# Block B's q and k: two of four x tiles by seven block products in place of eight

## The chip, the cores and the metric

The kernel runs on one core of a Trainium2 chip. The metric is the device time of one execution in microseconds (us), the median of several. Five engines work side by side, each in the order of its own queue: TensorE (PE; its weight loads are listed as PEld), VectorE (DVE), ScalarE (ACT), GpSimd (POOL) and SyncE (SP), which issues nearly all DMAs. PSUM has eight banks of 128 x 512 numbers here; PE writes into them, and ACT and DVE read them out.

## The reference

Two attention blocks, A and B, run on inputs of their own, and their outputs stand side by side. Both have a sequence of 2048, a width of 640 and 32 heads of 20.

```
qkv = (x @ wqkv).reshape(B, S, 3, H, Dh)          # both blocks
A:  logits over 8 dilated neighbours (idx = pos - 2*w), softmax, weighted sum, @ wo
B:  softmax(q @ k^T * Dh**-0.5) @ v over all 2048 positions, @ wo
out = concatenate([a, b], axis=-1)
```

The change touches only block B's q and k: `x @ wqkv[:, :1280]`, which is 10 feature blocks of 128 by 2048 positions, with a contraction of 640.

## The kernel before

All numbers are float32. For a product in float32 precision each operand is split into a high part (rounded) and a low part (operand less high part), and each chunk of 128 of the contraction takes three matmuls, `PASSES`: high by high, high by low, low by high. A split is one ACT copy (the high part) and one subtraction, mostly on DVE (`a_split`, line 217).

The stages follow one another on PE:

1. Block A's q and k (lines 597 to 692). The first x tile is done plainly, tiles 1 to 3 partly by Strassen's algorithm (`a_four`, line 264; the sums of x are `x_sums` on POOL, line 363). The last feature columns of A are done in `a_narrow` (line 633): four groups for each x tile. `a_narrow(2)` and `a_narrow(3)` are the last eight groups ahead of the stage that is changed.
2. **Block B's q and k** (line 760): for five pairs of feature blocks (`MS` gives their order, k's first), for four x tiles of 512 positions, for the two blocks of the pair: one group of 15 matmuls into one PSUM bank (5 chunks by 3 passes). 40 groups, 600 matmuls. Each result is copied by ACT into the high half of a pair tile, DVE subtracts for the low half, and SP stores the pair tile (512 KB) to `qb_d` or `kb_d`.
3. v of A and of B (line 1298), beside it the row maxima of B's scores.
4. The main loop (line 1456): B's scores, exponentials and weighted sums, with an order of the work written out by hand (`ORDER`), and A's output product where its rows are ready (token `H`). The last part is B's output product, by Strassen's algorithm.

POOL computes block A's attention the whole way through (`a_attention`, line 479): units that multiply, add and reduce rows which SP fetches from `qa_d`, `ka_d` and `va_d` into the four buffers with the tag `akv`. How many units stand in the program beside a group of PE's is set by `a_pace` (line 566): a count of estimated POOL time (`gp.us`) is kept within `AHEAD` of a wanted time, in this stage `A_SLOW * QK_US * groups`. This decides only the order in each queue; POOL itself runs ahead as long as its data are there. The units of scores stop until the first rows of v are known (`v_rows`).

`tick()` (line 112) is called once for each group; `after(n, fn)` puts work `n` ticks later. Tiles are asked for by tag; a tag has a fixed number of buffers (`bufs`), and whoever writes into a new tile waits until the old one in that buffer has been read for the last time. Tags that matter here: `big` (4, the x tiles), `w` (4, split weights), `stg` (3, raw weights), `pa` and `pb` (3 each, pair tiles), `akv` (4), `ao` and `raw` (3 each, A's rows on their way out), `rb`, `vb` (2 each), `aot` (1), `r` (4). `keep_in_program_order` keeps each engine's instructions in the order of the program.

x tiles 0 and 1 of block B are loaded ahead of the stage (`b_load`), tile 2 between `a_narrow(2)` and `a_narrow(3)`, tile 3 in three pieces after the first groups (`loads`). Later in the stage come the raw x of the v stage (`xv_ask`, into `vb` and `aot`) and v's weights (`wide_pieces`), and in the last eight groups the first loads of B's k and q from `kb_d` and `qb_d` (`b_pieces`).

Of the kernel before, what the change touches and what calls it, by code (L numbers as in the profile page):

```python
# [17 lines left out]
S = 2048  # L18
# [4 lines left out]
KC = 5  # L23
# [27 lines left out]
QK_US = 3.42  # L51
# [24 lines left out]
def attention_pair(ctx, tc, xa, wqk_a, wv_a, wo_a, xb, wqk_b, wv_b, wo_b, oa, ob):  # L76
# [498 lines left out]
    XB, WB = [], []  # L575
# [88 lines left out]
    def w_ask(n):  # L664
        w, fns = m_pieces(MS[n])
        WB.append(w)
        fns[0]()
# [12 lines left out]
    for n in (1, 2, 3):  # L680
        for r in range(2):
            a_four(n, r, step)
        if n == 1:
            a_narrow(1)
    wait[0] = 3
    w_ask(0)
    w_ask(1)
    p_next[:] = "bbbaaa"
    b_load(1)
    a_narrow(2)  # L690
    b_load(2)
    a_narrow(3)
    wait[0] = 2
    ones = [sb.tile([128, 16 * VC + 11], F32, tag=tag, bufs=3 if tag == "raw" else 2, name="ve")
            for tag in ("raw", "rb", "raw", "rb")]
    for t in ones:
        dve.memset(t, 1.0)
    w, loads = x_pieces(xb, 3)
    XB.append(w)


# [33 lines left out]
    def x_raw(c):  # L735

        out = []
        for a, b in PAIRS:
            raw = p_tile()[:, :(b - a) * 512].rearrange("p (k c) -> p k c", c=512)
            sp.dma_start(raw, (xa, xb)[c // 4][a * 128:b * 128, c % 4 * 512:c % 4 * 512 + 512].rearrange("(k p) c -> p k c", p=128))  # L740
            out.append((a, b, raw))
        return out
# [3 lines left out]
    def xv_ask():  # L746

        t = columns(0)
        XV.append((t, None))
        for j, (tag, bufs) in enumerate((("vb", 2), ("aot", 1))):  # L750
            raw = sb.tile([128, 1280], F32, tag=tag, bufs=bufs, name="xr")
            for k, c0, n, r in ((2 * j, 0, 2, raw[:, :1024].rearrange("p (k c) -> p k c", c=512)), (4, 256 * j, 1, raw[:, 1024:].unsqueeze(1))):
                c = r.shape[2]
                sp.dma_start(r, xa[k * 128:(k + n) * 128, c0:c0 + c].rearrange("(k p) c -> p k c", p=128))
                u, m = t[k // (KC - 1)], k % (KC - 1)
                after(8, a_split, u[:, 0, m:m + n, c0:c0 + c], u[:, 1, m:m + n, c0:c0 + c], r)

    groups = 0
    gp.us = 0.0
    for m in range(0, 10, 2):  # L760
        nxt = []
        for n in range(4):
            for j in range(2):
                p = next(banks)
                for k in range(KC):
                    for i, (wi, xi) in enumerate(PASSES):
                        pe.matmul(p, WB[j][:, wi, k], chunk(XB[n], xi, k), start=(k == 0 and i == 0),
                                  stop=(k == KC - 1 and i == 2))
                c = MS[m + j]
                o = (0, 1) if c < KC else (1, 0)  # L770
                pt = p_pair(F32R)
                act.copy(pt[:, o[0]], p)
                dve.tensor_tensor(pt[:, o[1]], p, pt[:, o[0]].bitcast(F32), ALU.subtract)
                after(1, sp.dma_start, dst_b(c, n).rearrange("t p c -> p t c"), pt.bitcast(F32))
# [3 lines left out]
                if m < 8 and n == (m == 0):  # L778
                    w, loads = m_pieces(MS[m + 2 + len(nxt)])
                    nxt.append(w)  # L780
                elif m == 6 and (n, j) == (2, 0):
                    xv_ask()
                elif m == 6 and (n, j) == (3, 0):
                    w0, loads = wide_pieces(wv_a[0])
                elif m == 8:
                    g8 = 2 * n + j
                    if g8 == 1:
                        k_loads, q_loads = b_pieces(0)
                    elif 1 < g8 < 6:
                        k_loads.pop(0)()  # L790
                        if g8 == 5:
                            xraw = x_raw(1)
# [9 lines left out]
                if groups > 4:  # L802
                    a_pace(A_SLOW * QK_US * groups)
        WB = nxt
# [472 lines left out]
    def x_parts(c, raws, second=gp):  # L1277
# [6 lines left out]
        for a, b, raw in raws:  # L1284
            u, m = t[a // (KC - 1)], a % (KC - 1)
            hi, lo = (u[:, x, m:m + b - a] for x in range(2))
            act.copy(hi, raw)
            if c not in (2, 3):
                second.tensor_tensor(lo, raw, hi.bitcast(F32), ALU.subtract)

# [244 lines left out]
```

## Time and profile before

| | us |
|---|---|
| median of 3 runs (1719.35 to 1720.92) | 1720.4 |
| the profiled execution | 1720.44 |
| its span, first to last instruction | 1718.4 |
| stage of B's q and k, first to last matmul's start of the next stage (137.29 to 274.21) | 136.92 |
| PE busy | 1708.8 |
| DVE busy | 1458.6 |
| ACT busy | 1335.6 |
| POOL busy | 1316.5 |

The span leaves 2.0 us of the execution's time outside it. Nearly all instructions are recorded under line 71, because one helper emits them; so groups are told apart by the tiles that they write and read: `ps_st<-xn,w` is a matmul into PSUM from an x tile and a weight tile, `xn<-stg,xn` the subtraction that makes an x tile's low part, `akv<-akv,aq` the multiplication that opens a score unit of block A, `w<-stg,w` the low part of weights. Times in a timeline are from the span's start.

### The profile page before, as it was taken

To read this page: it belongs to the slowest core of one execution; us is meant where nothing else is said; L and a number is where in the kernel's file an instruction comes from. 1 tells how busy PE (TensorE), PEld (TensorE's weight loads), DVE (VectorE), ACT (ScalarE), POOL (GpSimd) and SP (SyncE) were. 2 spreads that over 40 slices of the span, in tenths; PEclk is the share of its full clock that TensorE was granted. 3 is DMA by queue.
4 is the path that set the end of the run, shared out by engine and by line. 5 is a ranking of instruction groups with operands and counts; after the bars stand their busy time and mean duration, and the time that the engine had idled before them with its cause. 6 is when DMAs were issued, how large, how long until landed. Compare 5 with 4: busy or idle time off the path is not lost.

```text
span 1718.4 us, 34879 instructions
## 1 busy us (share of the span) xinstructions
PE 1708.8 (99%) x12627; PEld 990.3 (58%) x12627; DVE 1458.6 (85%) x1975; ACT 1335.6 (78%) x2637; POOL 1316.5 (77%) x1175
## 2 busy tenths in 40 slices
PE   9999999999999999999999999999999999999999
PEld 8888889999544544444444444444444445434459
DVE  8554334889899999999999999999999999999537
ACT  6213224232799999999999999999999999999972
POOL 4110990589999999999999999999999973486352
PEclk9999999999999999999999999999999999999999
DMA  6548979966843364345436345542644532111123
GB/s 196 183 158 265 327 259 281 304 196 207 221 138 104 102 185 132 102 128 161 129 112 168 115 124 129 171 136 84 164 135 117 140 99 75 40 49 41 34 73 118
DMA packets 207844, 253.53 MB, mean 148 GB/s; under 512 B 89788, under 2 KB 131004, under 8 KB 206680
## 3 DMA queue, kind: packets, MB, share of 16 engines
q1 hardware_dynamic: 206232, 249.67, 48.8%
q8 instruction: 99, 1.62, 0.4%
q10 hardware_dynamic: 1440, 1.64, 0.3%
q14 instruction: 73, 0.60, 0.1%
HBM read 183.70 MB, written 67.53 MB: 146 GB/s over the span
## 4 chain that ended last, share of the span: by engine, by line
PE 82%; POOL 9%; DVE 3%; ACT 2%; DMA 2%; issue 1%; SPq 0%; POOLq 0%; DVEq 0%; ACTq 0%
PE ps_st L71 82%; POOL akv L71 5%; DVE mx L71 3%; ACT stg L71 1%; POOL braw L71 1%; POOL ao L71 1%; POOL xn L71 1%; POOL ww L71 0%; DMA stg<-wqk_a 0%; DMA stg<-xa 0%; DVE wg L71 0%; POOL al L71 0%; SPq L71 0%; DMA stg<-wo_a 0%; ACT more L71 0%
## 5 line engine op out<-in xcount | busy, mean ns | idle before, releaser
L71 DVE TENSOR_REDUCE mx<-ps_st 128x1 f32<-128x512 f32 (+1 forms) x1504 | 1228.6, 876 | 56.1 <-PE ps_st L71 46.7
L71 ACT ACTIVATE stg<-ps_st 128x512 f32<-128x512 f32 x2000 | 1046.1, 630 | 41.4 <-PE ps_st L71 28.0
L71 PE MATMUL ps_st<-bk,bq 60*128 60x512 f32 x2048 | 553.7, 436 | 0.7 <-DVE mx L71 0.3
L71 PE MATMUL ps_st<-bq,bk 62*128 62x512 f32 x2048 | 549.0, 432 | 1.0 <-ACT e L71 0.9
L71 PE MATMUL ps_st<-stg,vb 128*32 128x512 f32 x4000 | 531.6, 604 | 0.4
L71 PEld LDWEIGHTS ps_st<-bq,bk 62*128 62x128 f32 x2048 | 274.9, 184 | 399.2 <-ACT stg L71 241.8
L71 POOL TENSOR_TENSOR braw<-braw,more 128x512 f32<-128x512 f32 x224 | 289.4, 1292 | 58.8 <-ACT more L71 56.6
L71 PEld LDWEIGHTS ps_st<-bk,bq 60*128 60x128 f32 x2048 | 257.1, 184 | 108.2 <-DVE mx L71 61.3
L71 POOL TENSOR_TENSOR akv<-akv 128x640 f32<-128x640 f32 (+3 forms) x304 | 284.0, 934 | 14.4
L71 POOL TENSOR_TENSOR akv<-akv,aq 128x1280 f32<-128x1280 f32 x64 | 188.2, 2941 | 76.5 <-PE ps_st L71 76.5
L71 PEld LDWEIGHTS ps_st<-stg,vb 128*32 128x32 f32 x4000 | 79.5, 108 | 143.5 <-issue 70.4
L71 POOL TENSOR_TENSOR akv<-akv,al 128x1280 f32<-128x1280 f32 x64 | 151.5, 2367 | 0.7 <-DMA akv<-va_d 0.5
L71 ACT COPY more<-ps_st 128x512 f32<-128x512 f32 x224 | 137.6, 614 | 2.7 <-PE ps_st L71 2.2
L71 ACT COPY ro<-ps_st 128x320 f32<-128x320 f32 (+2 forms) x130 | 52.6, 453 | 108.7 <-PE ps_st L71 76.9
L71 DVE TENSOR_TENSOR ro<-ps_st,ro 128x320 f32<-128x320 f32 (+1 forms) x112 | 61.9, 574 | 86.2 <-PE ps_st L71 78.2
L71 PE MATMUL ps_st<-ww,xn 64*128 64x320 f32 (+1 forms) x1392 | 123.9, 307 | 0.0
L71 PEld LDWEIGHTS ps_st<-ww,xn 64*128 64x128 f32 (+1 forms) x1392 | 117.7, 185 | 3.6 <-ACT stg L71 0.7
L71 PE MATMUL ps_st<-xn,w 128*128 128x512 f32 x480 | 115.9, 390 | 0.0
L71 PE MATMUL ps_st<-ww,aot 64*128 64x320 f32 x960 | 100.4, 309 | 1.5 <-POOL aot L71 1.5
L71 PEld LDWEIGHTS ps_st<-xn,w 128*128 128x128 f32 x480 | 90.0, 188 | 19.5 <-DVE xn L71 0.2
L71 PEld LDWEIGHTS ps_st<-ww,aot 64*128 64x128 f32 x960 | 90.4, 186 | 8.0 <-POOL aot L71 2.0
L71 ACT CAST stg<-ps_st 128x512 fp32r<-128x512 f32 x40 | 23.4, 589 | 76.1 <-PE ps_st L71 76.1
(116 smaller groups left out, 1329.4 us busy)
## 6 DMA issues: line engine op xcount, KB each, us to landing
akv<-ka_d SPq DMA_DIRECT2D x128, 320.0 KB
akv<-va_d SPq DMA_DIRECT2D x128, 320.0 KB
kb_d<-stg SPq DMA_DIRECT2D x20, 512.0 KB
qb_d<-stg SPq DMA_DIRECT2D x20, 512.0 KB
bk<-kb_d SPq DMA_DIRECT2D x16, 640.0 KB
bq<-qb_d SPq DMA_DIRECT2D x64, 160.0 KB
stg<-xb SPq DMA_DIRECT2D x16, 512.0 KB
rb<-s_d SPq DMA_DIRECT2D x128, 64.0 KB
```

The costliest lines, as they stand in the source:

```text
L71: return self.tc.keep_in_program_order(op(*a, **k))
```

## The change

The first two x tiles are done as before (`b_plain`). The third and fourth, n = 2 and 3, are done together for each pair of feature blocks. Their product is a 2 by 2 one: feature blocks j = 0, 1 by x tiles 2, 3, with a contraction of two halves, chunks 0 and 1 and chunks 2 and 3. Strassen's algorithm in Winograd's form needs seven products of such blocks instead of eight; chunk 4 is added plainly to four of the results.

- `x_pair` loads tiles 2 and 3 into the four `akv` buffers right behind the loads of tile 1, ahead of `a_narrow(2)`, with eight DMAs. Six and eight ticks later the parts that are needed as such are split. Nine ticks later POOL makes four sums of x, each 128 x 1024, in place in the raw tiles; ten to twelve ticks later these are split into `T2`, `T3`, `T1` and `T4` (`t_split`, two ACT copies and two DVE subtractions of 128 x 512 each), which lie in tags that are free in this stage (`homes`).
- For each pair of feature blocks DVE makes four sums of the raw weights (`s_sums`, 128 x 256 each) one tick after the pair's first group, and a tick later four splits follow (`s_parts`: four ACT copies, four DVE subtractions, 128 x 256).
- `b_four` gives the products in four steps that take the place of the four groups: 12, 15, 15 and 12 matmuls, 54 in place of 60. DVE adds them up (seven additions that read PSUM), ACT copies out the first product and then makes four high parts, and DVE subtracts for four low parts (both operands in SBUF).
- The weights of a pair are asked for together (`w_get`), and their raw tiles stay for the sums.
- A's units on POOL are put into the program from the seventh group on instead of the fifth, at `QK_US` 3.25 instead of 3.42 a group.
- The constant tiles `ones` for the v stage are set by POOL after the stage instead of by DVE ahead of it.
- The raw x of the v stage's first two tiles is loaded into `akv` buffers, in the first and the sixth of the last eight groups; before, into `vb` and `aot` four groups earlier, and into pair tiles.

```diff
-QK_US = 3.42
+QK_US = 3.25
...
+    def w_get(n):
+
+        for m in MS[n:n + 2]:
+            w = sb.tile([128, 2, KC, 128], F32R, tag="w", bufs=4, name="w")
+            raw = sb.tile([128, KC, 128], F32, tag="stg", bufs=3, name="stg")
+            sp.dma_start(raw, wqk_b[m])
+            WB.append((w, raw))
+            after(wait[0], a_split, w[:, 0], w[:, 1], raw)
...
+    def x_pair():
+
+        t2, t3 = columns(2), columns(3)
+        XB.extend([t2, t3])
+        r2, r3 = (akv_raw(xb, n) for n in (2, 3))
+        (x11, x21), (x12, x22) = ((r[0][3], r[2][3]) for r in (r2, r3))
...
+        def t_split(n, raw):
+            hi, lo = TB[n]
+            for k in range(2):
+                act.copy(hi[k], raw[:, k])
+                dve.tensor_tensor(lo[k], raw[:, k], hi[k].bitcast(F32), ALU.subtract)
+        for p in r2:
+            after(6, put, t2, p)
+        for p in (r3[1], r3[2], r3[3]):
+            after(8, put, t3, p)
+        after(8, homes)
+        for out, a, b in ((x11, x12, x11), (x12, x22, x12), (x22, x22, x11), (x21, x21, x22)):
+            after(9, pool, out, a, b, ALU.subtract)
+        for n, (at, raw) in {2: (10, x22), 3: (10, x12), 1: (11, x11), 4: (12, x21)}.items():
+            after(at, t_split, n, raw)
+
+    def s_sums(j0, j1):
+
+        (a11, a12), (a21, a22) = ((r[:, :2], r[:, 2:4]) for r in (j0, j1))
+        for out, a, b, op in ((a22, a21, a22, ALU.add), (a21, a11, a21, ALU.subtract), (a11, a22, a11, ALU.subtract), (a12, a12, a11, ALU.subtract)):
+            dve.tensor_tensor(out, a, b, op)
+
+    def s_parts(j0, j1):
+
+        for n, r in (("2", j0[:, :2]), ("4", j0[:, 2:4]), ("3", j1[:, :2]), ("1", j1[:, 2:4])):
+            a_split(*(u.rearrange("p (k c) -> p k c", c=128) for u in SB[n]), r)
...
     p_next[:] = "bbbaaa"
     b_load(1)
+    x_pair()
     a_narrow(2)
-    b_load(2)
     a_narrow(3)
...
-    for t in ones:
-        dve.memset(t, 1.0)
...
+        def one():
+            act.copy(tile_of(0, 2), prod("11", "11"))
+            p = prod("S2", "T2")
+            plus(p, low(0, 2), tile_of(0, 3))
+
+        def second():
+            plus(prod("12", "21", (0, 2)), low(0, 2), low(0, 2))
+            high(0, 2)
+            p = prod("S3", "T3")
+            plus(p, low(0, 3), tile_of(1, 2))
+            done(0, 2)
+
+        def third():
+            p = prod("S1", "T1")
+            plus(p, low(0, 3), low(0, 3))
+            plus(p, low(1, 2), tile_of(1, 3))
+            plus(prod("S4", "22", (0, 3)), low(0, 3), low(0, 3))
+            high(0, 3)
+            done(0, 3)
+
+        def fourth():
+            plus(prod("22", "T4", (1, 2)), low(1, 2), low(1, 2))
+            high(1, 2)
+            plus(prod(None, None, (1, 3)), low(1, 3), low(1, 3))
+            done(1, 2)
+            high(1, 3)
+            done(1, 3)
...
+                if n < 2:
+                    b_plain(MS[m + j], n, W[j][0])
+                else:
+                    four = four or b_four(m, W)
+                    four.pop(0)()
+                if (n, j) == (0, 0):
+                    after(1, s_sums, *raws)
+                    after(2, s_parts, *raws)
                 tick()
...
-                if groups > 4:
+                if groups > 6:
                     a_pace(A_SLOW * QK_US * groups)
...
+                    if g8 == 0:
+                        t = columns(0)
+                        XV.append((t, None))
+                        for p in akv_raw(xa, 0):
+                            after(4, put, t, p)
...
+    for t in ones:
+        gp.memset(t, 1.0)
```

133 lines of the change are left out of this document (88 added, 45 removed).

## The prediction

> **What bounds the kernel now.** I read the page first, then the chain that ended last, then the stage by engine and by groups.
>
> ```profile
> PE 1708.8 (99%) x12627; PEld 990.3 (58%) x12627; DVE 1458.6 (85%) x1975; ACT 1335.6 (78%) x2637; POOL 1316.5 (77%) x1175
> POOL 4110990589999999999999999999999973486352
> ```
>
> ```profile
> 35.18 340.46 PE ps_st L71 x2316
> ...
> 380.79 2.94 POOL akv L71
> ...
> 542.90 1.56 POOL aot L71
> 544.50 35.54 PE ps_st L71 x286
> ```
>
> PE is busy throughout. The chain runs on PE alone from 35 to 376 us, so each microsecond taken out of PE's queue there moves what follows; from 381 to 544 us it runs over POOL, which therefore must not come later than PE does. The stage itself, 40 groups of 15 matmuls:
>
> ```profile
> 137.29:274.21 136.92, 136.92 (x603) 112.53 (x602) 51.04 (x67) 37.94 (x63) 84.11 (x80) 1.00 0.85 285
> ```
>
> ```profile
> L71 DVE TENSOR_TENSOR stg<-ps_st,stg 128x512 fp32r<-128x512 f32 x39 | 26.7, 688 | 59.1 <-ACT stg L71 59.1
> L71 DVE TENSOR_TENSOR w<-stg,w 128x640 fp32r<-128x640 f32 x8 | 10.9, 1360 | 8.4 <-ACT w L71 8.4
> L71 DVE TENSOR_TENSOR xn<-stg,xn 128x1024 fp32r<-128x1024 f32 x4 | 4.9, 1226 | 11.8 <-ACT xn L71 11.8
> L71 DVE TENSOR_TENSOR xl<-stg,xl 128x512 fp32r<-128x512 f32 x3 | 2.1, 686 | 0.3 <-ACT xl L71 0.3
> L71 DVE TENSOR_TENSOR xl<-xr,xl 128x256 fp32r<-128x256 f32 x2 | 0.8, 418 | 0.0
> L71 ACT CAST xn<-stg 128x1024 fp32r<-128x1024 f32 x4 | 4.2, 1055 | 12.1 <-DMA stg<-xb 12.1
> ...
> L71 DVE MEMSET ve<- 128x347 f32 x4 | 1.4, 348 | 0.1
> ```
>
> PE never stops here, at the full clock (1.00): 136.92 / 600 = 0.2282 us a matmul. DVE has 51 of 137 us of work, ACT 38, POOL 84.
>
> **PE's part.** Each pair of feature blocks loses 6 of 120 matmuls, the stage 30: 30 x 0.2282 = **6.85 us off**. A pair then takes 114 x 0.2282 = 26.0 us: 13.7 for four plain groups, 12.3 for the four steps.
>
> **What DVE costs beside POOL.** Most new DVE instructions have both operands in SBUF. The rows show what such a one does beside a running POOL instruction, and what POOL's sums take with and without DVE:
>
> ```profile
> 14.78 2.56 POOL L71 TENSOR_TENSOR rw<-rw 128x1024 f32<-128x1024 f32 x1 [12.55 <-DMA rw<-wqk_a]
> 15.29 2.60 DVE L71 TENSOR_TENSOR wd<-rw,wd 128x512 fp32r<-128x512 f32 x1 [0.21 <-ACT wd L71]
> ...
> 28.68 6.17 POOL L71 TENSOR_TENSOR stg<-stg 128x512 f32<-128x512 f32 x4 [1.16 <-DMA ka_d<-ro]
> 29.13 6.20 DVE L71 TENSOR_TENSOR wg<-stg,wg 128x256 fp32r<-128x256 f32 x6
> 57.13 5.75 POOL L71 TENSOR_TENSOR stg<-stg 128x512 f32<-128x512 f32 x4 [22.28 <-DVE xn L71]
> ```
>
> ```profile
> L71 POOL TENSOR_TENSOR rw<-rw 128x1024 f32<-128x1024 f32 x4 | 11.3, 2821 | 14.0 <-DMA rw<-wqk_a 12.6 <-DVE wc L71 0.7 <-DVE wd L71 0.7
> L71 DVE TENSOR_TENSOR wg<-stg,wg 128x256 fp32r<-128x256 f32 x4 | 4.8, 1234 | 0.0
> ```
>
> ```profile
> L71 POOL TENSOR_TENSOR xn<-stg,xn 128x1024 fp32r<-128x1024 f32 x2 | 4.8, 2402 | 0.0
> ```
>
> The 128x512 subtraction at 15.29 takes 2.60 us in place of 0.69: it ends at 17.89, 0.55 after POOL's 17.34. So it waits for the end of POOL's instruction. A 128x256 one takes 1.23 in place of 0.42, a 128x640 one 1.36 in the stage. A sum of 128x1024 on POOL takes 2.40 alone and 2.82 with DVE at work.
>
> **The first pair, where the sums of x are made.** The second product of step one needs T2 and S2. PE starts the step here:
>
> ```profile
> 150.94 2.88 PE L71 MATMUL ps_st<-xn,w 128*128 128x512 f32 x12
> ```
>
> The third matmul of product two, which takes S2's low part, is due at 150.94 + 8 x 0.2282 = 152.8. What stands ahead of S2:
>
> ```profile
> 127.15 1.40 SPq L71 DMA_DIRECT2D stg<-xb  x3
> 128.64 8.43 SPq L71 DMA_DIRECT2D ka_d<-ro  x4
> 137.12 1.48 SPq L71 DMA_DIRECT2D stg<-xb  x3
> ```
>
> ```profile
> 134.89 1.05 ACT L71 CAST xn<-stg 128x1024 fp32r<-128x1024 f32 x1 [0.18 <-DMA stg<-xb]
> 135.85 0.61 ACT L71 CAST xl<-stg 128x512 fp32r<-128x512 f32 x1
> 136.37 1.18 ACT L71 COPY ro<-ps_st 128x256 f32<-128x256 f32 x4
> 142.26 1.05 ACT L71 CAST xn<-stg 128x1024 fp32r<-128x1024 f32 x1 [4.71 <-DMA stg<-xb]
> 143.55 1.06 ACT L71 CAST xn<-stg 128x1024 fp32r<-128x1024 f32 x1 [0.23 <-DMA stg<-xb]
> ```
>
> SP issues the eight loads from 128.6 on, 0.47 us each, ahead of stores that waited for ACT until 136.4 anyway: nothing on the path. ACT is done with tile 1 at 136.5 and with three copies of A's rows at 137.4, then makes the high part of x11 until 138.5; DVE's low part ends at 139.7. From there POOL and DVE take turns:
>
> - POOL's first sum 139.7 to 142.5, then DVE's low part of x21 (1.2); second sum to 145.3;
> - DVE's low part of x22, which the third sum overwrites, to 146.5; third sum to 149.3, fourth to 152.1;
> - of the weights' four sums one fits in at 149.3, three come after 152.1: 3 x 0.42, 153.4; the second group's subtraction 0.69, 154.1;
> - T2's and T3's low parts, which stand ahead in DVE's queue, 4 x 0.69: 156.8; S2's low part 0.42: **157.3**.
>
> PE waits 157.3 - 152.8 = **4.5 us**. ACT's parts fit beside it, and the eight PSUM banks hold the plain groups until DVE comes to them. Lower bound: POOL and DVE don't hold each other up. Sums at 2.40, end of the third 146.9, the weights' sums and the second subtraction long done, then 0.61 for ACT, 4 x 0.69 and 0.42: 150.7, no wait, 0. Upper bound: tile 2's loads took 6.4 us from issue (137.12) to the second cast (143.55). If tiles 2 and 3 follow tile 1 (135.85) at 8.4 us for a whole tile, x22, two thirds into tile 3, is there at 149.6. Then come the second sum (152.4), its low part (153.6), third and fourth sum (159.2) and the 5.2 us from there to S2: 164.4, a wait of 11.6. I take 4.5: the 2.60-us row is the same kind of pair of instructions, and the loads stand one behind the other without SP's pause of 137.
>
> **The later pairs.** For each, DVE has 4 plain subtractions and 7 additions that read PSUM (11 x 0.69 = 7.6), 8 of 128x256 at 1.23 (9.8), 4 of 128x512 and the two of new weights at 1.36 (8.2): 25.6 of 26.0 us. This is the cover of the whole new DVE work, and it is thin. S2 is ready 3.4 + 1.3 (first group and its eviction) + 4 x 1.23 + 0.69 + 1.23 = 11.6 us into a pair, and needed at 13.7 + 8 x 0.2282 = 15.5: 3.9 us to spare, so I take 0. Bounds: 0, and, with 128x512 and 128x640 ones at 1.78 as where DVE met POOL's long sums, 7.6 + 9.8 + 10.7 = 28.1, 2.1 us over in each of four pairs, 8.4.
>
> ```profile
> L71 DVE TENSOR_TENSOR wc<-rw,wc 128x512 fp32r<-128x512 f32 x2 | 3.5, 1781 | 0.0
> ```
>
> ACT has, for a pair, 4 plain copies, one more of PSUM, 4 high parts, 4 of S and 2 of weights. Even at the 1.06 us of the longer casts these 15 would take 15.9 of 26 us. Cost 0.
>
> **A's units on POOL.**
>
> ```profile
> 160.92 0.77 SPq L71 DMA_DIRECT2D aq<-qa_d  x1
> ...
> 168.47 2.94 POOL L71 TENSOR_TENSOR akv<-akv,aq 128x1280 f32<-128x1280 f32 x1 [76.45 <-PE ps_st L71]
> ...
> 242.60 2.96 POOL L71 TENSOR_TENSOR akv<-akv,aq 128x1280 f32<-128x1280 f32 x1
> ...
> 305.62 0.74 POOL L71 TENSOR_TENSOR al<-al,am 128x256 f32<-128x256 f32 x1 [48.09 <-DVE am L71]
> ```
>
> The first fetch now stands behind the third step: 137.3 + 13.7 + 42 x 0.2282 + 4.5 + 1.5 (the last addition and subtraction on DVE, 0.69 each) = 166.6, and POOL starts 7.55 later, at 174.1 (5.6 later than before). Twelve units fit ahead of a pause of 48.09 us, so this costs 0; without the pause, the chain from 381 to 544 us would be late by that much. The four memsets of `ones` (1.4 us on DVE) move into the same pause: 0. `QK_US` changes only the program's order: 0.
>
> **The sum.** 1720.44 (profiled run, at the median of 1720.4) - 6.85 + 4.5 = **1718.1 us**, 0.13% less. A measurement of this kernel tells about 0.2%, 3.4 us, from no change.
>
> **The rivals.**
>
> *The sums are in time* (the lower bound of the first pair): 1720.44 - 6.85 = 1713.6. For it: DVE and ACT are idle more than half of the stage, and two plain x tiles stand ahead. Against it: the 2.60-us row. Chance 0.35, some waits of 1 to 3 us included.
>
> *DVE becomes the bound of every pair* (slower): 1718.1 + 8.4 = 1726.5. It decides from 26.0 us of DVE work a pair on; I count 25.6. Against it: POOL's short additions let DVE in sooner than its sums of 2.8 us do. Chance 0.11.
>
> *The v stage waits for its x tile* (slower). `xa`'s loads go into buffers of units nine and ten, so SP stands still until POOL has ended these; before, they were issued at 238.49 and cast at 264.57. Ten units took 242.60 - 168.47 = 74.1 us; from 174.1 on, 248.2. Landing (6.5 us, as 127.15 to 133.65 for tile 1) and the last piece's cast and subtractions (1.06, 1.23 and 0.42) take 9.2, and PE needs the tile at 274.21 - 6.85 + 4.5 = 271.9: it decides from 262.7 on. Behind SP stand then the stores of three plain results and the last piece of v's weights; six pair tiles cover the stores.
>
> ```profile
> 133.65 1.05 ACT L71 CAST xn<-stg 128x1024 fp32r<-128x1024 f32 x1 [2.87 <-DMA stg<-xb]
> ...
> 238.49 2.41 SPq L71 DMA_DIRECT2D xr<-xa  x4
> 264.57 1.05 ACT L71 CAST xn<-xr 128x1024 fp32r<-128x1024 f32 x1
> ```
>
> Some 35 additional DVE instructions fall into these 74 us. Six of them cost POOL 6.17 - 5.75 = 0.42 at 28.68, 0.07 each: 250.7, no wait. A large one costs 2.82 - 2.40 = 0.42: 262.9, at the edge. At 0.63 each (half more) it is 270.3, and the time 1718.1 + 7.6 = 1725.7. Chance 0.10. The Trainium skill (page "SBUF — State Buffer", section "Who interferes with whom") holds that a DVE instruction with two SBUF inputs and a GpSimd one that reads SBUF lock each other out for a whole instruction; by that POOL would lose each one's full 0.42 to 0.69 us, some 18 us in all, and end at 266.2, 3.5 us late: 1721.6. The row of 0.07 speaks against the full price, the 2.60-us row for the lock itself.
>
> **How the numbers follow.** The forecast, a first wait of 2.5 to 7 us, has 0.44; its own times are 1716.1 to 1720.6. Faster by over 0.2% (below 1717.0) is 0.33 of the first rival and 0.05 of the forecast: 0.38. Slower by over 0.2% (above 1723.8) is the two slower rivals but for 0.01: 0.20. Within 0.2% is the rest, 0.42. The range goes from the full gain (1713.2 with the scatter of the runs) to 1724.5, a first wait near its upper bound (1713.6 + 10.9), and leaves out the larger part of the slower rivals.
>
> **What would show it.** In the changed profile: 570 matmuls in the stage at 0.228 us; a gap on PE near 152 us ahead of the matmuls from S2 and T2, ended by DVE's low part of S2, none or little in the later pairs; DVE's 128x256 sums beside POOL's 128x1024 ones well over 0.42 us; POOL's first unit near 174. No gap there, or one of over 8 us, makes the forecast wrong, and so does a gap at the start of the v stage behind `xn<-xr`, or PE waiting for POOL in the main loop.

## The result: 21 us slower

| | us |
|---|---|
| before, median of 4 runs (1719.35 to 1720.92) | 1720.13 |
| after, median of 4 runs (1738.33 to 1742.24) | 1741.57 |
| ratio, 95% interval | 1.0121, 1.0109 to 1.0134 |
| the profiled execution after, its span | 1741.62, 1739.8 |
| predicted (range) | 1718.1 (1713.2 to 1724.5) |

The page of the changed kernel, PE's and POOL's part, and the row of the stage from its first matmul to the first of v:

```profile
PE 1713.3 (98%) x12597; PEld 990.1 (57%) x12597; DVE 1531.1 (88%) x2061; ACT 1346.2 (77%) x2672; POOL 1333.1 (77%) x1183
...
POOL 4112884379999999999999999999999983486352
```

```profile
136.98:281.84 144.86, 136.37 (x572) 109.53 (x570) 109.78 (x139) 47.52 (x92) 86.76 (x76) 0.96 0.71 244
```

PE has 30 matmuls fewer and is yet busy 4.5 us longer: the clock that it was granted in the stage is 0.96, not 1.00. The stage takes 144.86 us instead of 136.92; PE stands still for 8.5 us of it (144.86 less 136.37). DVE is busy for 109.78 of it instead of 51.04. PE's timeline of the changed kernel, its waits in brackets:

```profile
153.72 0.50 PE L71 MATMUL ps_st<-tx,sx 128*128 128x512 f32 x1 [1.57 <-ACT sx L71]
154.94 0.50 PE L71 MATMUL ps_st<-tx,sx 128*128 128x512 f32 x1 [0.72 <-DVE tx L71]
157.08 2.08 PE L71 MATMUL ps_st<-tx,sx 128*128 128x512 f32 x4 [1.64 <-DVE sx L71]
158.96 2.76 PE L71 MATMUL ps_st<-xn,w 128*128 128x512 f32 x6
161.51 1.48 PE L71 MATMUL ps_st<-xl,w 128*128 128x512 f32 x3
162.79 1.63 PE L71 MATMUL ps_st<-tx 128*128 128x512 f32 x6
...
213.89 1.88 PE L71 MATMUL ps_st<-tx,sx 128*128 128x512 f32 x4 [1.81 <-DVE sx L71]
...
243.32 1.18 PE L71 MATMUL ps_st<-tx,sx 128*128 128x512 f32 x4 [1.56 <-DVE sx L71]
...
281.84 0.41 PE L71 MATMUL ps_st<-ww,xn 128*128 128x320 f32 x1 [1.04 <-ACT xn L71]
285.38 1.61 PE L71 MATMUL ps_st<-ww,xn 128*128 128x320 f32 x6 [3.12 <-DVE xn L71]
...
312.23 3.57 PE L71 MATMUL ps_st<-ww,xn 64*128 64x320 f32 x24 [1.84 <-ACT ro L71]
```

The clock behind the first stop (PEclk is the third number from the end of a row):

```profile
157.00:159.00 2.00, 1.92 (x5) 1.53 (x6) 2.00 (x6) 1.27 (x3) 0.00 (x0) 0.50 0.00 0
...
161.00:163.00 2.00, 2.00 (x6) 1.52 (x5) 1.24 (x3) 0.00 (x0) 0.00 (x0) 0.51 0.93 241
163.00:165.00 2.00, 2.00 (x10) 1.60 (x10) 0.85 (x2) 1.45 (x2) 0.00 (x0) 1.00 0.95 362
```

From these times and the starts of the pairs (a pair without waits is 114 x 0.2282 = 26.0 us):

| | pair 1 | 2 | 3 | 4 | 5 | stage | start of v |
|---|---|---|---|---|---|---|---|
| before | 27.4 | 27.4 | 27.4 | 27.4 | 27.4 | 136.92 | 17.69 |
| after | 33.49 | 26.02 | 29.67 | 27.85 | 27.83 | 144.86 | 30.39 |

"Start of v" is from v's first matmul to the first 64-row block (291.90 before, 312.23 after); pair five's 27.83 holds the 1.04 us for which PE waited for v's x tile. The block comes 20.33 us later: 6.85 saved, 14.8 lost in the stage (8.5 as waits, 6.3 as slower matmuls), 12.7 lost at the start of v, 0.3 gained ahead of the stage. Behind it only 0.85 of the 21.18 us between the two profiled executions is left. So there are three places to explain: pair one, pairs three to five, and the start of v.

DVE's groups in pairs two and three of the changed kernel (busy us, mean ns, idle time before them):

```profile
L71 DVE TENSOR_TENSOR w<-stg,w 128x640 fp32r<-128x640 f32 x4 | 9.4, 2373 | 9.0 <-ACT w L71 9.0
L71 DVE TENSOR_TENSOR stg<-ps_st,stg 128x512 f32<-128x512 f32 x11 | 7.1, 681 | 1.4 <-PE ps_st L71 1.4
L71 DVE TENSOR_TENSOR stg<-stg 128x256 f32<-128x256 f32 x8 | 6.5, 812 | 0.2
L71 DVE TENSOR_TENSOR stg<-stg 128x512 fp32r<-128x512 f32 x7 | 6.2, 904 | 1.8 <-ACT stg L71 1.4
L71 DVE TENSOR_TENSOR sx<-stg,sx 128x256 fp32r<-128x256 f32 x4 | 6.0, 1547 | 0.0
L71 DVE TENSOR_TENSOR stg<-ps_st,stg 128x512 fp32r<-128x512 f32 x8 | 5.5, 684 | 2.3 <-ACT stg L71 2.2
L71 DVE TENSOR_TENSOR tx<-stg,tx 128x256 fp32r<-128x256 f32 x4 | 2.8, 747 | 0.0
```

Two things stand in these rows. The additions that read PSUM take 681 ns, as they do without POOL; the instructions with both operands in SBUF take 747 to 1547 ns at 128x256, where 0.42 us is the price alone. And DVE stood still for 9.0 us behind ACT's casts of new weights, which were themselves late.

### The profile page after: what moved, and what is told of

Its sections match the earlier page's. It is cut to its first block, busy times and chain, and to the rows that moved or that the text cites. A ratio compares the mean times of both kernels' runs of the same rounds, so it can differ in the third digit from the quotient of the medians.

```text
span 1739.8 us, 34971 instructions
## 1 busy us (share of the span) xinstructions
PE 1713.3 (98%) x12597; PEld 990.1 (57%) x12597; DVE 1531.1 (88%) x2061; ACT 1346.2 (77%) x2672; POOL 1333.1 (77%) x1183
## 3 DMA queue, kind: packets, MB, share of 16 engines
q10 hardware_dynamic: 1440, 1.64, 0.3%
## 4 chain that ended last, share of the span: by engine, by line
PE 78%; DVE 8%; DMA 5%; POOL 4%; issue 2%; ACT 1%; SPq 1%; DVEq 0%; ACTq 0%; POOLq 0%
PE ps_st L71 78%; DVE mx L71 4%; DVE stg L71 2%; POOL akv L71 2%; DMA kb_d<-stg 1%; DMA stg<-wqk_b 1%; POOL braw L71 1%; ACT stg L71 1%; SPq L71 1%; DMA xr<-xb 1%; DMA xr<-xa 0%; DMA va_d<-ro 0%; DMA stg<-wqk_a 0%; DMA stg<-xa 0%; POOL ao L71 0%
## 5 line engine op out<-in xcount | busy, mean ns | idle before, releaser
L71 POOL TENSOR_TENSOR akv<-akv 128x640 f32<-128x640 f32 (+3 forms) x304 | 289.3, 952 | 14.4
L71 PE MATMUL ps_st<-ww,xn 64*128 64x320 f32 (+1 forms) x1392 | 128.1, 311 | 10.1 <-DVE xn L71 5.0
L71 POOL TENSOR_TENSOR ao<-ao,akv 128x640 f32<-128x640 f32 x48 | 75.0, 1563 | 2.0
L71 PE MATMUL ps_st<-xn,w 128*128 128x512 f32 x300 | 75.2, 398 | 0.0
L71 PEld LDWEIGHTS ps_st<-xn,w 128*128 128x128 f32 x300 | 57.9, 193 | 12.5
```

The source lines that it names most:

```text
L71: return self.tc.keep_in_program_order(op(*a, **k))
```

## The experiments

"Theory A" in the expectations: lateness is handed on through queues that are worked off in order. "Theory B": POOL and DVE lock each other out, which makes DVE too slow. "Theory C": the new loads and buffers alone. The results of all 18 runs; the pairs, the stage and the start of v are read from one profiled execution of each:

| run | us | ratio, 95% interval | pairs 1 to 5 | stage | start of v |
|---|---|---|---|---|---|
| e_plain | 1721.5 | 0.9997 to 1.0022 | 27.4 each | 136.82 | 19.30 |
| e_dvesums | 1740.3 | 1.0092 to 1.0151 | 32.5 26.0 31.2 27.9 27.2 | 144.71 | 29.81 |
| e_put6 | 1738.1 | 1.0079 to 1.0138 | 32.4 26.0 28.0 31.0 26.0 | 143.46 | 28.52 |
| e_early | 1745.6 | 1.0123 to 1.0182 | 30.4 26.0 30.5 36.0 26.0 | 148.93 | 29.90 |
| e_gap | 1735.5 | 1.0072 to 1.0112 | 27.4 28.9 31.3 31.9 34.1 | 153.48 | 17.69 |
| e_late22 | 1747.0 | 1.0138 to 1.0179 | 33.3 26.0 26.0 26.0 30.6 | 141.91 | 33.96 |
| e_spool | 1749.0 | 1.0150 to 1.0190 | 31.5 37.1 26.8 29.3 26.7 | 151.42 | 28.65 |
| e_best1 | 1746.2 | 1.0134 to 1.0168 | 27.4 39.3 27.9 32.1 26.0 | 152.76 | 27.53 |
| e_psum | 1727.5 | 1.0026 to 1.0058 | 30.9 26.0 26.2 26.0 26.0 | 135.18 | 25.72 |
| e_memset | 1745.9 | 1.0130 to 1.0171 | 33.0 26.0 28.2 31.1 32.1 | 150.34 | 28.96 |
| e_best2 | 1725.6 | 1.0013 to 1.0040 | 27.0 26.2 30.7 26.0 26.0 | 135.88 | 21.93 |
| e_best3 | 1718.2 | 0.9985 to 1.0002 | 26.9 26.0 26.8 26.0 27.4 | 133.03 | 20.09 |
| e_best4 | 1720.9 | 0.9998 to 1.0016 | 27.1 26.0 26.0 26.0 26.0 | 131.14 | 24.57 |
| e_best6 | 1717.5 | 0.9977 to 0.9995 | 26.2 26.0 26.5 26.0 26.0 | 130.80 | 20.65 |
| e_best7 | 1716.8 | 0.9974 to 0.9992 | 26.0 26.0 26.0 26.0 27.4 | 131.43 | 18.28 |
| e_qd | 1719.6 | 0.9988 to 1.0006 | 27.4 each | 136.82 | 17.69 |
| e_wget | 1736.7 | 1.0066 to 1.0125 | 33.2 26.0 26.0 33.3 26.0 | 144.52 | 28.09 |
| e_last | 1741.2 | 1.0092 to 1.0151 | 34.1 26.0 29.7 27.9 27.4 | 145.15 | 27.83 |

### The staging without the products (e_plain)

```diff
-        for p in (r3[1], r3[2], r3[3]):
+        for p in r3:                      # and no sums, T or S
...
-                if n < 2:
+                if n < 4:
```

> The changed kernel's loads, buffers and order of the work, but all four x tiles done plainly (no sums of x or of weights, no products of sums; the output is the full one). Theory A (lateness is passed on through the queues of DVE, ACT and SP by Strassen's additional work): the stage of q and k is free of waits again, 600 matmuls x 0.228 = 136.9 us, and the time from the stage's end to the first block of maxima, 17.7 us before and 31.6 us after the change, falls to 18 to 24: 1720 to 1727 us. Theory C (the loads in the akv buffers, the weights asked for in pairs and the memsets on POOL cost the time by themselves): the start of v stays at 30 us or more, 1733 us or more.

1721.5 us, the stage free of waits, the start of v 1.6 us longer. Theory C falls: of the 21 us the staging has 2.0 by the medians (1719.5 for the kernel before in these runs), and 3.8 at most by the interval.

### The order in pair one (e_dvesums, e_put6, e_early)

```diff
e_dvesums:
-            after(9, pool, out, a, b, ALU.subtract)
+            after(9, dve.tensor_tensor, out, a, b, ALU.subtract)
e_put6:
-            after(8, put, t3, p)
+            after(6, put, t3, p)
e_early:
+        after(5, s_sums, *raws0)
+        after(9, s_parts, *raws0)
...
-                if (n, j) == (0, 0):
-                    after(1, s_sums, *raws)
-                    after(2, s_parts, *raws)
+                if m < 8 and (n, j) == (3, 0):
+                    after(1, s_sums, *[r for _, r in WB])
+                if m < 8 and (n, j) == (3, 1):
+                    after(1, s_parts, *[r for _, r in WB])
```

> x's four sums on DVE instead of POOL, nothing else changed. If POOL's sums and DVE's work lock each other out in the first pair (A), S2 and T2 come some 3 us earlier, PE's stops near 153 us shrink from 7.5 us (clock loss included) to 0 to 3.5, and the time is 1734 to 1738. If it is DVE's amount of work that is late there (B), four more DVE instructions of 1.2 us each make it later: first pair 33.5 us or more, 1741 to 1746.

> Only the split of the last x22 part (and its two neighbours) two ticks earlier, so that it stands in ACT's queue ahead of the copies of A's rows that wait for the stores of rows before them. If the wait of ACT for those stores (2.76 us) is what makes the sums late (A), the first pair shrinks from 33.5 to 28 to 31 us and the time is 1736 to 1739. If the sums are late by the lock of DVE and POOL alone, the first pair stays at 33 us and the time at 1741.

> The sums and parts of a pair's weights are put into the program earlier: for the first pair four ticks ahead of its first group, for the others behind the third step of the pair before. The work is the same to the instruction. If order and lateness are the cause (A), pairs two to five take 26.0 to 26.5 us each (in place of 26.0, 29.7, 27.9 and 26.6) and the first pair 28 to 32: 1731 to 1737 us. If DVE's amount of work beside POOL bounds each pair (B), nothing moves by more than 1 us: 1740 to 1743.

In six kernels that leave pair one as the change has it (the changed one, e_late22, e_spool, e_memset, e_wget, e_last) it took 31.5 to 34.1 us. The 32.5 and 32.4 of e_dvesums and e_put6 lie in this scatter, so neither shows an effect by itself: moving the sums to DVE frees it of the lock and gives it 5.0 us more to do, and ACT's wait for stores that stood behind the eight loads, which e_put6 was to spare x22, is there but does not decide; ACT's timeline of the changed kernel:

```profile
142.95 0.69 ACT L71 COPY ro<-ps_st 128x256 f32<-128x256 f32 x2 [2.76 <-DMA ka_d<-ro]
...
143.85 1.05 ACT L71 CAST xn<-xr 128x1024 fp32r<-128x1024 f32 x1
```

e_early's 30.4 us is below the scatter. But it speaks against order alone: with the weights' sums and parts ahead of their pair, pairs three and four became longer (30.5 and 36.0), because the eight instructions now fell into the third and fourth step, where DVE was behind already.

### A stop's price (e_gap)

```diff
+                if j == 0 and n == 1 and m in (2, 4, 6, 8):
+                    for _ in range({2: 6, 4: 7, 6: 8, 8: 10}[m]):
+                        act.copy(WB[0][:, 1], WB[0][:, 1].bitcast(F32))
```

> The kernel before the change, with stops of PE put in on purpose: after the third group of pairs two to five ACT copies the low part of the first block's weights onto itself 6, 7, 8 and 10 times (0.73 us each), so that PE's fifth group has to wait about 1.0, 1.8, 2.5 and 4.0 us; output and all other work are unchanged. If a stop costs a drop of the granted clock beside its own length, the clock falls to about 0.50 for some us after the longer ones and not after the shortest: 120 matmuls of such a pair take their 27.4 us, the stop and 1.5 to 3 us more, and the whole 1732 to 1738 us. If the drops in the changed kernel have another cause, the clock stays at 1.00: 1728 to 1731 us.

PE's timeline, the four stops and, for the first two, where the next group starts:

```profile
179.49 2.56 PE L71 MATMUL ps_st<-xn,w 128*128 128x512 f32 x10 [1.25 <-ACT w L71]
...
182.59 2.91 PE L71 MATMUL ps_st<-xn,w 128*128 128x512 f32 x12
...
209.15 3.83 PE L71 MATMUL ps_st<-xn,w 128*128 128x512 f32 x10 [2.01 <-ACT w L71]
...
213.83 2.92 PE L71 MATMUL ps_st<-xn,w 128*128 128x512 f32 x12
...
241.17 4.00 PE L71 MATMUL ps_st<-xn,w 128*128 128x512 f32 x10 [2.76 <-ACT w L71]
...
275.17 4.06 PE L71 MATMUL ps_st<-xn,w 128*128 128x512 f32 x10 [4.89 <-ACT w L71]
```

```profile
210.00:212.00 2.00, 2.00 (x7) 1.54 (x6) 2.00 (x2) 0.21 (x1) 1.92 (x2) 0.53 0.87 336
212.00:214.00 2.00, 2.00 (x7) 1.60 (x6) 0.10 (x1) 0.00 (x0) 1.92 (x2) 0.61 0.30 115
214.00:216.00 2.00, 2.00 (x10) 1.61 (x10) 1.35 (x2) 1.21 (x2) 1.76 (x4) 1.00 0.00 0
```

Behind the stop of 1.25 us, 13 matmuls take 3.10 us; behind the one of 2.01 they take 4.68, with a clock of 0.53 to 0.61. Behind 2.76 and 4.89 the clock is as low, and the 13 matmuls take 4.52 and 4.59 (to 245.69 and 279.76). So a stop costs its own length and, if the clock falls, about 1.5 us more, whatever its length. In the changed kernel, behind three stops in a row, the 13 matmuls from 157.08 took 5.71 us instead of 2.97.

### POOL out of the way, or loaded with more (e_late22, e_spool, e_best1)

```diff
e_late22:
-                if groups > 6:
+                if groups > 22:
e_spool (pairs two to five):
-            dve.tensor_tensor(out, a, b, op)                 # s_sums
+            gp.tensor_tensor(out, a, b, op)
-            a_split(...)                                     # s_parts
+            act.copy(hi, r); gp.tensor_tensor(lo, r, hi.bitcast(F32), ALU.subtract)
e_best1: e_spool, e_dvesums, e_put6, e_memset (below), and the first pair's
+        after(5, s_sums, *raws0)
+        after(9, s_parts, *raws0)
```

> The changed kernel with block A's units put into the program from the 23rd group on instead of the seventh, so that POOL rests during pairs two and three. If the lock between POOL's units and DVE's instructions with two SBUF operands makes S2 late (B), these take 0.69 us (128x512) and 0.42 us (128x256) there in place of 1.1 and 0.8 to 1.75, and pair three falls from 29.7 to 26.0 to 26.5 us. If late raw weights alone do it (A), pair three stays at 28.5 us or more. POOL's units then come some 50 us later, as long as the pause they had, so the start of v should be no better than 31.6 us: 1738 to 1760 us in all.

> The changed kernel with the sums and the low parts of the weights for pairs two to five on POOL instead of DVE (eight instructions of about 0.7 us a pair). By the lock (B) DVE loses the eight instructions that suffer most from it, and pairs three to five take 26.0 to 26.8 us each (after the change 29.7, 27.9, 26.6); the first pair (33.5) and the start of v (31.6) stay: 1734 to 1738. If S2 is late by the raw weights (A), it becomes later by POOL's own queue, where a unit of 7 us stands ahead: pairs of 29 us or more and 1742 us or more.

> Five edits together: x's sums on DVE, the last x22 split two ticks earlier, the first pair's weight sums and parts ahead of the stage, the later pairs' on POOL, and the memsets of the constant tiles 14 ticks later (behind block A's tenth and eleventh units on POOL). If the lock and the order of the queues are the whole loss, the first pair takes 26 to 27.5 us, the later ones 26.0 to 26.8, the start of v 18 to 24: 1714 to 1722 us. If the change is bound by something else, it stays above 1730 us.

DVE's groups in pairs two and three of e_late22, where POOL rests until 228.26:

```profile
L71 DVE TENSOR_TENSOR stg<-stg 128x256 f32<-128x256 f32 x8 | 3.4, 422 | 0.2
L71 DVE TENSOR_TENSOR w<-stg,w 128x640 fp32r<-128x640 f32 x4 | 3.2, 820 | 0.2 <-ACT w L71 0.2
...
L71 DVE TENSOR_TENSOR sx<-stg,sx 128x256 fp32r<-128x256 f32 x4 | 1.5, 416 | 0.0
```

The 128x256 ones are back at 416 to 422 ns, the 128x640 ones at 820 instead of 2373, and pairs two to four take 26.0 us. But with the units gone, their loads are gone from SP's queue too, and DVE waited 0.2 us for weights instead of 9.0: the run takes away both causes. And the units come 51 us later, into the start of v (33.96). e_spool does not free DVE for nothing: POOL's sums stand behind a unit in its queue, and PE waited 6.10 us in pair two for ACT's part of S2. e_best1 adds the first pair's edits, and these hold (27.4 us), but pair two is worse still. My expectation for both was wrong.

### One operand in PSUM (e_psum)

```diff
+        p = [next(banks) for _ in range(3)]
+        s1, s3, s2, s4, c21 = ...                            # quarters and halves of p
+        act.copy(c21, a21)
+        for out, a, b, op in ((s1, c21, a22, ALU.add), (s3, a11, c21, ALU.subtract), (s2, s1, a11, ALU.subtract), (s4, a12, s2, ALU.subtract)):
+            dve.tensor_tensor(out, a, b, op)
...
+        def last(p, j, n):                                   # the last addition of each result
+            F[j, n] = p
+            plus(p, low(j, n), p)                            # high and low half are made from p
```

> The changed kernel with the same count of DVE additions and subtractions, but each new one of the later steps has one operand in PSUM instead of SBUF: ACT copies one quarter of the raw weights into PSUM, the four sums of the weights are written into PSUM and split from there, and the last addition of each of the four results is written back into its own bank, from which the high and the low half are made. If the lock between DVE's instructions with two SBUF operands and POOL's units makes S2 late (B), pairs three to five take 26.0 to 26.6 us each with POOL's units running beside them as before, the first pair 29 to 32, and the whole 1727 to 1735 us. If it is the lateness of the raw weights alone (A), or DVE's count of instructions, pair three stays above 28 us and the time at 1738 or more.

DVE's groups in pairs two and three, POOL's units beside them as before (the first at 178.48, after the change 177.68):

```profile
L71 DVE TENSOR_TENSOR w<-stg,w 128x640 fp32r<-128x640 f32 x4 | 6.1, 1534 | 10.6 <-ACT w L71 10.6
L71 DVE TENSOR_TENSOR ps_st<-ps_st,stg 128x512 f32<-128x512 f32 x8 | 5.3, 688 | 0.0
...
L71 DVE TENSOR_TENSOR ps_st<-stg,ps_st 128x256 f32<-128x256 f32 x4 | 1.7, 428 | 0.1
...
L71 DVE TENSOR_TENSOR sx<-ps_st,sx 128x256 fp32r<-128x256 f32 x4 | 1.7, 420 | 0.9 <-ACT sx L71 0.9
```

The same additions and subtractions take 428 and 420 ns at 128x256 and 688 at 128x512, whatever POOL does. The weights are as late as before (DVE waits 10.6 us for them), and still pairs two to five take 26.0 to 26.2 us. The whole is 14 us faster than the changed kernel. So the lock on the new instructions is needed for this loss; in this run weights as late as before don't make it. The splits of the weights themselves (`w<-stg,w`) keep both operands in SBUF, and their 1534 ns. The Trainium skill, page "SBUF — State Buffer", section "Who interferes with whom", says that a DVE instruction with at most one SBUF input does not contend with GpSimd; these rows agree.

### The start of v (e_memset, e_last) and the late weights alone (e_wget)

```diff
e_memset:
-        gp.memset(t, 1.0)
+        after(14, gp.memset, t, 1.0)
e_last:
-                if n < 2:
+                if n < 2 or m == 8:                          # and no sums for m == 8
e_wget:
-                if m < 8 and (n, j) == (1, 0):
+                if m < 8 and (n, j) == (0, 1):
                     w_get(m + 2)
```

> The changed kernel with the four memsets of the constant tiles 14 ticks later, so that block A's tenth and eleventh units no longer stand behind them on POOL. If these units beside the splits of v's x tile are what stops PE at the start of v, they run from about 256 to 271 us now, the start of v falls from 31.6 to 22 to 26 us, and the time to 1733 to 1737 us. If v's weights and x come late by themselves (through the raw weights' three buffers and SP), the start of v stays above 29 us: 1739 to 1743.

> The changed kernel with the fifth pair done plainly and nothing else. If the late start of v (30.4 us in place of 17.7) is the last pair's additional work on DVE, ACT and SP, it falls to 18 to 21 us, while the first four pairs keep 33.5, 26.0, 29.7 and 27.9 us and the fifth takes 27.4: 1730 to 1734 us. If it is handed on from the pairs before it, or comes from block A's last two units on POOL, it stays at 25 us or more: 1737 or more.

> The changed kernel with the next pair's weights asked for one group earlier and nothing else; the lock stays. In the changed kernel DVE stood 9.0 us in pairs two and three waiting for these weights, and its own work there was 23.5 us a pair. If S2 is late by the two together (waiting and locked work over 26 us), earlier weights alone take pairs three and four from 29.7 and 27.9 to 26.0 to 27.0 us: 1735 to 1738. If the lock alone does it, they stay above 27.5: 1740 or more.

I had held block A's last two units, delayed by the memsets, to be what stops PE at the start of v. e_memset does not bear it out: the eleventh of the twelve units (the expectation calls it the tenth) moved from 281.35 to 255.76, while the twelfth's additions still came behind the memsets, at 286.33. The start of v fell by 1.4 us only, and pair five rose to 32.1, since POOL now met DVE there; DVE's timeline:

```profile
255.78 3.48 DVE L71 TENSOR_TENSOR stg<-stg 128x512 fp32r<-128x512 f32 x1
...
264.06 4.01 DVE L71 TENSOR_TENSOR stg<-stg 128x512 fp32r<-128x512 f32 x2
```

One subtraction of 0.69 us took 3.48, two took 4.01. e_last refutes both this guess and the next one. Its fifth pair is plain, both units end at 274.6, and v's splits run at the price that they have alone (1.23 us); still the start of v takes 27.8 us. PE waits 8.96 us at 309.90, and SP's timeline shows from where the delay comes:

```profile
257.67 8.18 SPq L71 DMA_DIRECT2D qb_d<-stg  x4
265.90 0.50 SPq L71 DMA_DIRECT2D stg<-wv_a  x1
...
297.04 5.79 SPq L71 DMA_DIRECT2D bq<-qb_d  x4
...
304.29 2.44 SPq L71 DMA_DIRECT2D va_d<-ro  x4
```

SP stands until 265.85 with the stores of pair four's results, which DVE finishes 10.7 us after PE's last product of that pair (254.72 to 265.4); v's weights, v's raw x, the loads of B's q and at last the stores of v's rows, for which ACT waits, all come behind. The lateness of pair four is handed on. But it is not the whole of the late start: in e_psum pairs two to five are free, and the start of v still takes 25.72 us. e_wget shows the other half of the cause: with earlier weights alone pair three is free (26.01), pair four then takes 33.3, and pairs three to five together take the 85.3 us that they take in the changed kernel. How the loss falls on pairs three and four varies in any case: in e_put6 they take 28.0 and 31.0. The 1736.7 us of e_wget lie in the range that was expected, but not for its reason, since the pairs gained nothing and the start of v is 2.3 us shorter. So without the lock on the new instructions all later pairs are free though the weights are late (e_psum); with it, earlier weights only move the loss to the next pair. The lock is the necessary part, the late weights add to it.

### Putting it right (e_best2 to e_best7, e_qd)

```diff
e_best2: e_psum from pair two on, e_dvesums, e_put6, e_memset, and for pair one
+    after(3, s_sums0, *[r for _, r in WB])                   # sums in SBUF, POOL rests here
+        after(9, s_parts, *[r for _, r in WB])
e_best4: e_best2 without e_memset, with e_wget
e_best3: e_best4 with e_last
e_best6, e_best7: e_best4 and e_best3 with, and e_qd: the kernel before with
-                            q_loads.pop(0)()
+                            after(6, q_loads.pop(0))
```

> Together: one operand of each new DVE instruction in PSUM from the second pair on; the first pair's sums of weights right behind the weights' split, x's sums on DVE and the last x22 split two ticks earlier (there POOL rests, so nothing locks); the memsets 14 ticks later. By the lock and the queues' order as the whole loss: first pair 26 to 27.4 us (27.4 with 1.08 us of waiting when these first-pair edits ran together), the others 26.0 to 26.6, start of v 18 to 24: 1713 to 1722 us. If there is a further cause, 1726 or more.

> As the last combined kernel (one operand in PSUM, the first pair's order), but the next pair's weights are asked for one group earlier, the fifth pair is done plainly (its third and fourth x tile in four groups of 15 matmuls, so 24 matmuls fewer than before the change in place of 30), and the memsets stand where the change had them. If late raw weights are what is left of pair three's loss (4.9 us) and the burst of the last pair's results is what delays the stores ahead of the 64-row blocks (4.2 us), the first four pairs take 27.0, 26.0, 26.0 to 26.5 and 26.0, the fifth 27.4, the start of v 17.7 to 19.5: 1720.2 - 5.5 + 1.0 + 0 to 2.5 = 1715.5 to 1718. If the start of v is late for another reason (the raw x in akv buffers, SP's order), it stays at 21 us or more and the time at 1719 or more.

> The same with the fifth pair by seven products as well. Pair three 26.0 to 26.5 as there. If the burst of the last pair's results is what delays the start of v, this one keeps 21 to 23 us there: 1720.2 - 6.85 + 1.0 + 3.5 to 6 = 1718 to 1721, above the other. If not, it is 1.4 us below the other.

> The kernel with all five pairs by seven products and one operand in PSUM, and the first four loads of B's q six ticks later in SP's queue, behind the first stores of v's rows. In the run without this the stage of q and k took 131.1 us in place of 136.9, and PE then waited 6.81 us ahead of the 64-row blocks: ACT's copies of v's rows waited for stores that stood on SP behind those loads. If SP's order is that cause, the stores are issued near 277 in place of 286, ACT goes on behind its splits at 286.6, the block starts at 287 to 288 in place of 292.1, and the time is 1715 to 1717.5 us. If the loads of the raw x into the akv buffers are the cause, the block stays at 291 or later: 1719.5 or more.

> The same later loads, with the fifth pair done plainly. By SP's order: the wait of 2.33 us and the lower clock behind it go, the block starts at 287.2 in place of 289.7: 1714.5 to 1716.5 us. Otherwise 1718 as without it.

> The kernel before the change with these four loads six ticks later and nothing else. There PE does not wait ahead of the block (291.90, ACT's copies end at 291.6), so nothing is expected: 1719 to 1721 us. If it gains too, what the two other runs gain by it is not owed to the shorter stage.

e_best2 brought pair one to 27.0 but left 30.7 in pair three, where PE waited for a weight's low part: the weights were late, and their two splits, which keep both operands in SBUF, took 4.75 us beside POOL. In e_psum, with the same instructions in the later pairs, these two took 1.69 us, so that its free pair three was in part luck. e_best4 asks for the weights earlier, and all later pairs take 26.0: the stage is 131.14 us, the change's whole promise but 1.1 us. Yet the time is that of the kernel before. The gain is lost at the start of v, in one wait; PE's, SP's and ACT's timelines of e_best4:

```profile
292.13 3.69 PE L71 MATMUL ps_st<-ww,xn 64*128 64x320 f32 x23 [6.81 <-ACT ro L71]
```

```profile
278.25 4.87 SPq L71 DMA_DIRECT2D bq<-qb_d  x4
...
286.11 2.05 SPq L71 DMA_DIRECT2D va_d<-ro  x4
```

```profile
282.85 1.05 ACT L71 CAST xn<-xr 128x1024 fp32r<-128x1024 f32 x1 [5.87 <-DMA xr<-xa]
...
291.65 1.66 ACT L71 COPY ro<-ps_st 128x320 f32<-128x320 f32 x4 [5.04 <-DMA va_d<-ro]
```

PE waits 6.81 us for ACT's copies of v's rows; these wait for stores (va_d) that SP issues at 286.11, behind four loads of B's q and the last pair's stores. With the loads six ticks later the block starts at 287.70 instead of 292.13 (e_best6), and with a plain fifth pair at 286.65 (e_best7). The start of v falls from 24.57 to 20.65 and 18.28 us. In e_best6 ACT is done with its splits at 282.90, not at the 286.6 of the expectation, and still waits 4.33 us for the stores; so part of that wait stays. In the kernel before, the same edit does nothing (e_qd), so this gain belongs to the shorter stage. **e_best7 beats both kernels**: 1716.8 us, ratio 0.9983 (0.9974 to 0.9992), 3.2 us or 0.17% under before; e_best6 at 0.9986 does so too, and the two can't be told apart. The expectations for e_best2 (at most 1722), e_best3 (1718) and e_best7 (1716.5) were too good by 3.6, 0.2 and 0.3 us.

## Why the prediction was wrong, step by step

- **PE's part, 6.85 us: right.** Without waits a pair takes 26.0 us (pair two of the changed kernel, and all but the first of e_best4).
- **The first pair, 4.5 us: right in its mechanism, too small.** S2's low part was forecast for 157.3, and the matmuls that need it started at 157.08. The waits of 1.57, 0.72 and 1.64 us are 3.93 in all. The pair lost 7.5: 2.7 more went by the clock, which fell to 0.50 behind the stops (this term was missing), and 0.8 are not assigned. That POOL and DVE take turns is not the whole cause: without POOL's sums (e_dvesums) the pair lost 6.4 still. It takes the edits together to free it (26.0 to 27.4 us in e_best1 to e_best7).
- **The eight loads ahead of the stores, "nothing on the path": wrong in its reason.** ACT waited 2.76 us for these stores (142.95), with the cast of x22 behind it. What that cost was not to be seen: e_put6 moved pair one by less than its scatter.
- **The later pairs, "so I take 0": the step that failed.** The sum let DVE begin the weights' sums 4.7 us into a pair, right behind the first group, and had S2 ready at 11.6, 3.9 us early. In pair two that is so: the sums begin 4.9 us in, and PE does not wait. In pair three, which begins at 196.49, the sums begin 10.8 us in, and PE waits for S2's low part until 17.4 us; DVE's timeline of the changed kernel:

```profile
192.37 5.02 DVE L71 TENSOR_TENSOR w<-stg,w 128x640 fp32r<-128x640 f32 x2 [4.60 <-ACT w L71]
...
207.25 4.90 DVE L71 TENSOR_TENSOR stg<-stg 128x256 f32<-128x256 f32 x4
...
212.68 2.17 DVE L71 TENSOR_TENSOR sx<-stg,sx 128x256 fp32r<-128x256 f32 x2
```

DVE stood 4.60 us for pair three's weights, took 5.02 us for their two splits (0.82 each without POOL, e_late22) and then had pair two's additions to work off. The four sums took 4.90 us beside POOL; in pair two, before POOL's first unit at 177.68, they took 1.80. The amount of work was not what failed: the seven groups shown come to 43.5 us for two pairs, 22 a pair where the prediction put down 25.6 (the expectation of e_wget has 23.5, which the groups don't bear out). Its prices were too high for 128x512 (1.36, measured 0.90) and too low for 128x640 (1.36, measured 2.37). What the sum did not have is idle time in DVE's queue: 9.0 us in two pairs behind weights whose loads SP issued at 185.28, behind stores that had stood since 179.06 until DVE had made their low halves. Pairs three to five took 3.65, 1.84 and 1.82 us too long; 1.04 of the last is the wait for v's x tile. The rival of DVE as the bound came nearest, with a chance of 0.11, but its condition, 26.0 us of DVE work a pair, was not met; that its upper bound of 8.4 us lies near the 7.3 measured is luck.
- **The start of v, 12.7 us: in no part of the sum.** The rival that looked there blamed SP's wait for units nine and ten. The tenth was late indeed (it ended at 255.01, the first began at 177.68 and not at 174.1), but none of SP's waits between 255 and 312 us is for POOL. In its place the runs show two things: the lateness of the pairs before (e_last), and SP's order (e_best4, e_best6). Freeing the later pairs (e_psum) takes 4.7 of the 12.7 us away; in the combined kernels the four loads of B's q are worth 3.9 (24.57 to 20.65) and a plain fifth pair 2.4. The prediction followed no delay beyond the place at which it arose. PE's slack there was small to begin with: in the kernel before, the first of ACT's copies ends at 291.15 and the block starts at 291.90.
- **A's units, the memsets, at 0: right in the changed kernel as far as POOL's pause covers them**: the pause shrank from 48.09 to 29.56 us, and the main loop lost no more than 0.85 us. That was luck as well: the memsets do not move into that pause. They wait for PE, which still reads the sums of x in the buffers that they set, and so hold POOL still from 255.01 to 273.75 (in e_last, whose fifth pair reads none of these sums, they run at 255.64). This keeps POOL out of pair five's way: where the memsets are later (e_memset), pair five takes 32.1 us.

What is left open: what makes pair one scatter so (27.1 and 26.0 us in e_best4 and e_best7 with the same instructions, 31.5 to 34.1 above), and how the 12.7 us divide in the changed kernel itself, in which the loads of B's q were not moved alone. The lock at v's own splits has at most the 2.6 us by which e_last is shorter.

## What to carry to other kernels

Count the work that a change gives to an engine together with what that engine waits for in its own queue: 22 of 26 us are no cover if 4.5 us more are spent standing behind a late load. Where VectorE and GpSimd work side by side, give each VectorE instruction one operand in PSUM if a bank is free; the same arithmetic then costs what it costs alone. And follow each delay through the stores behind it to the next stage: here the start of the next stage lost 12.7 us; 4.7 of them went when the pairs were free, and four loads moved in SP's queue gave 3.9 more in the combined kernel.

## What the hardware did that was not expected

- The lock's price for one instruction ran from nothing to 2.8 us (0.69 against 3.48, above); in the rows shown only instructions with two SBUF operands pay it.
- A stop of PE can cost 1.5 us beyond its length, by a clock of 0.50 for some 3 to 4 us. Its length alone does not decide: behind 1.81 us (at 213.89 of the changed kernel) the clock fell, behind 2.29 us it did not; PE's timeline and the clock of e_late22 there:

```profile
266.00 1.18 PE L71 MATMUL ps_st<-tx,sx 128*128 128x512 f32 x4 [2.29 <-DVE sx L71]
```

```profile
264.00:266.00 2.00, 0.00 (x1) 0.00 (x1) 2.00 (x3) 0.37 (x1) 1.84 (x3) 1.00 0.35 99
266.00:268.00 2.00, 2.00 (x9) 1.66 (x10) 2.00 (x4) 0.08 (x1) 1.84 (x4) 1.00 0.87 298
```

The Trainium skill, page "TensorE: Matmul & The Clock Gate", section "What's actually happening", speaks of a free-running window of about 3.4 us; a stop that counts by how it lies to such a window would do this, and no run here shows the window itself.
